# Second MoE projection by Strassen's product for pairs of token tiles, with partial sums read midway

One Trainium2 chip, one of its cores. The metric is the device time of one execution in microseconds (us); lower is better. Faster or slower needs 2%. Engines: PE (TensorE) does the matmuls, ACT (ScalarE) exponentials and copies, DVE (VectorE) elementwise work and sums, POOL (GpSimd) the normalisation; SP is the queue that issues most of the DMAs, called the sync queue. PSUM is the memory that matmuls write to.

## The reference

Attention with RMS-normalised queries and keys (8 batches, 12 heads, 448 positions, 64 columns a head), then two projections with a gate between them on the 3584 tokens:

```python
q_n, k_n = (rmsnorm(q, g_q), rmsnorm(k, g_k))
scores = scale * np.matmul(q_n, k_n.transpose(0, 1, 3, 2))
attn = softmax(scores)                 # (written out in the reference)
x = (attn @ v), heads side by side     # 3584 x 768
h = x @ w_in                           # 768 x 2048
g = h * (1.0 / (1.0 + np.exp(-1.702 * h)))
return g @ w_out                       # 2048 x 768
```

## The kernel before

Everything is one stream per engine. While the program is built, a greedy list schedule (`_Order`) takes tasks with a modelled duration, a priority and dependencies, and fixes the order of the instructions on each engine. On the chip each engine then runs its list in that order and waits where a semaphore says so: PE does nothing else while it waits (in run e4 below it stood 2.70 us in front of one matmul, with the next ones behind it).

Names used below. F(b) is the first projection of batch b, 16 groups of 6 matmuls of 448 columns; each group is followed by a tanh on ACT and a gate on DVE. Y(b) is the second projection: 2 halves of 384 output columns, 16 matmuls of 384 columns for each token tile and half. Attention runs between them. The kernel takes 8 banks of PSUM: 4 for scores (two tiles of two banks each), 1 for attention's output, and 3, called w, which the MoE takes in turn.

```python
banks = [ps_w.tile([128, 512], FP32, tag=f"w{j}", name=f"w{j}") for j in range(3)]
...
def second(bp, tm, hf, c):
    if c == 0:
        ops[bp, tm, hf] = bank()[:, :HALF]
    for ko in range(4 * c, 4 * c + 4):
        nc.tensor.matmul(ops[bp, tm, hf],
                         lhsT=g_of[bp][:, ko, tm * 128:(tm + 1) * 128],
                         rhs=w_out_s[:, ko, hf * HALF:(hf + 1) * HALF],
                         start=(ko == 0), stop=(ko == MI - 1))

def take_out(bp, tm, hf):
    ...
    nc.scalar.mul(osb[:, hf * HALF:(hf + 1) * HALF], ps, 0.5)      # ACT, bank to SBUF
...
N_ATT, N_KZ, N_V, N_RAW, N_SQ, N_QKN = 3, 6, 6, 7, 2, 3            # depths of the rings
raw = ring("raw", N_RAW, [128, 2, 2, NS, D], FP32)                 # loaded q and k
```

## Time and profile before

| | before |
|---|---|
| median of the timed runs | 435.6 us |
| span of the profiled run | 434.0 us |
| PE busy / ACT busy / DVE busy | 421.0 / 318.5 / 216.8 us |
| second projection on PE | 896 matmuls at 162.6 ns, 145.7 us |
| PE idle by the list of waits after 60 us | none |

Spacing, used all through this text, is the time from the start of one matmul to the start of the next. A matmul's own duration in the profile (326 ns for 384 columns) is twice its spacing, so it overlaps the next one, and durations cannot be added. Where the spacing is larger than usual, PE waited.

### The profile page before, as it was taken

The page shows a single profiled execution, that of the slowest core. Times are in us where ns is not written, and L with a number is a line of the kernel's source. Part 1 is how long each engine was busy: PE and PEld are TensorE (multiplying, and loading weights), DVE is VectorE, ACT ScalarE, POOL GpSimd, SP SyncE. Part 2 cuts the span into 40 slices and gives each one's busy share as a digit, 9 for nine tenths or more (in the row PEclk, how much of TensorE's full clock was granted, in tenths as well). Part 3 has the DMA queues.
Part 4 walks back from the last instruction along what each step waited for, and adds up shares of the span by engine and source line. Part 5 has one row for each costly group of instructions (what it writes and reads, how often), then busy time and mean ns, then how long its engine had stood idle before and what let it go on. Part 6 is the DMA issues. An engine that isn't in the chain of part 4 may idle for free.

```text
span 434.0 us, 9991 instructions
## 1 busy us (share of the span) xinstructions
PE 421.0 (97%) x3962; PEld 249.5 (57%) x3962; DVE 216.8 (50%) x460; ACT 318.5 (73%) x472; POOL 180.5 (42%) x277
## 2 busy tenths in 40 slices
PE   6899899999999999999999999999999999999996
PEld 4558687655555555555555555555555555565563
DVE  5977978456575486735754255412551125404400
ACT  4897888769999999989987778766875466314411
POOL 5396753855849857655545454433010000000000
PEclk9999999999999999999999999999999999999999
DMA  9999999899787998677657933235112221021022
GB/s 208 240 253 245 266 251 249 197 257 231 142 216 157 257 255 207 168 175 194 169 120 155 234 98 79 62 85 122 34 33 58 58 76 22 12 72 38 0 74 73
DMA packets 97235, 63.38 MB, mean 146 GB/s; under 512 B 54052, under 2 KB 93732, under 8 KB 97188
## 3 DMA queue, kind: packets, MB, share of 16 engines
q1 hardware_dynamic: 89520, 56.05, 53.8%
q0 software_dynamic: 7296, 6.29, 8.9%
q8 instruction: 31, 0.51, 0.5%
q10 hardware_dynamic: 372, 0.40, 0.3%
q14 instruction: 16, 0.13, 0.1%
HBM read 45.61 MB, written 11.01 MB: 130 GB/s over the span
## 4 chain that ended last, share of the span: by engine, by line
PE 91%; ACT 4%; DMA 2%; DVE 1%; issue 1%; SPq 0%; ACTq 0%
PE w L860 34%; PE w L830 34%; PE o L620 12%; PE sc L599 10%; DMA raw<-in_k_dram 2%; ACT att L609 2%; ACT sq L482 1%; PE w L556 1%; DVE qk L563 0%; PE w L646 0%; DVE qk L560 0%; DVE g L852 0%; DVE obs L631 0%; SPq L475 0%; DVE xt L650 0%
## 5 line engine op out<-in xcount | busy, mean ns | idle before, releaser
L607 ACT ACTIVATE att<-sc 112x896 bf16<-112x896 f32 x168 | 146.1, 919 | 22.3 <-PE sc L599 22.0
L860 PE MATMUL w<-w_out_s,g 128*128 128x384 bf16 x896 | 161.4, 326 | 0.0
L830 PE MATMUL w<-xt,w_in_s 128*128 128x448 bf16 (+1 forms) x864 | 158.3, 332 | 0.0
L852 DVE SCALAR_TENSOR_TENSOR g<-th,w 128x448 bf16<-128x448 f32 x128 | 78.6, 617 | 67.2 <-ACT th L840 67.0
L860 PEld LDWEIGHTS <-g 128*128 128x128 bf16 x896 | 80.9, 98 | 52.4 <-issue 6.3
L830 PEld LDWEIGHTS <-w_in_s 128*128 128x128 bf16 x864 | 78.9, 98 | 52.9 <-issue 3.5
L533 POOL TENSOR_TENSOR row<-raw,rs 112x512 bf16<-112x512 f32 x87 | 90.5, 1063 | 20.5 <-DMA qk<-row 11.5
L620 PEld LDWEIGHTS <-att 112*128 112x128 bf16 x1536 | 70.5, 98 | 41.9 <-issue 20.4
L840 ACT ACTIVATE th<-w 128x448 f32<-128x448 f32 x128 | 69.7, 549 | 33.1 <-PE w L830 31.5
L620 PE MATMUL o<-vx,att 112*128 112x65 bf16 x1536 | 83.1, 195 | 0.8 <-ACT att L609 0.6
L546 POOL TENSOR_TENSOR vx<-vraw,ones 112x512 bf16<-112x512 f32 x42 | 43.7, 1042 | 88.4 <-PE o L620 78.3
L491 DVE TENSOR_REDUCE ssq<-sq 112x16 f32<-112x1024 f32 (+1 forms) x50 | 58.5, 1171 | 26.5 <-ACT sq L482 26.2
L871 ACT ACTIVATE osb<-w 128x384 f32<-128x384 f32 x56 | 27.6, 492 | 46.8 <-PE w L860 45.3
L630 DVE RECIPROCAL rcp<-o 112x4 f32<-112x4 f32 x96 | 17.2, 179 | 89.4 <-PE o L620 89.1
L599 PE MATMUL sc<-qk 64*128 64x448 bf16 (+1 forms) x432 | 54.3, 333 | 1.9 <-DVE qk L563 1.4
L482 ACT ACTIVATE sq<-raw 112x1024 f32<-112x1024 f32 (+1 forms) x46 | 47.6, 1043 | 5.5 <-DMA raw<-in_k_dram 2.5
L631 DVE TENSOR_TENSOR obs<-o,rcp 112x256 bf16<-112x256 f32 x96 | 40.7, 424 | 3.3
L574 ACT ACTIVATE qk<-qk,gG 128x448 bf16<-128x448 bf16 x36 | 24.5, 682 | 0.0
L599 PEld LDWEIGHTS <-qk 64*128 64x128 bf16 x432 | 13.0, 94 | 19.1 <-issue 12.3
L609 ACT ACTIVATE att<-sc 112x896 bf16<-112x896 f32 x24 | 20.5, 914 | 1.9 <-PE sc L599 1.8
L523 POOL TENSOR_TENSOR t<-rs 112x48 f32<-112x48 f32 x28 | 7.4, 265 | 23.8 <-DVE rs L512 22.5
L457 PE MATMUL w<-zeros,ident 128*128 128x256 bf16 x89 | 14.6, 297 | 1.4 <-POOL ident masks.py:199 1.4
(38 smaller groups left out, 110.3 us busy)
## 6 DMA issues: line engine op xcount, KB each, us to landing
raw<-in_q_dram SPq DMA_DIRECT2D x48, 224.0 KB, 4.3
vraw<-in_v_dram SPq DMA_DIRECT2D x48, 224.0 KB, 5.0
raw<-in_k_dram SPq DMA_DIRECT2D x47, 224.0 KB, 4.6
w_in_s<-in_moe_w_in_dram POOLq DMA_DIRECT2D x4, 768.0 KB, 16.1
w_out_s<-in_moe_w_out_dram POOLq DMA_DIRECT2D x4, 768.0 KB, 20.9
out_dram<-osb SPq DMA_DIRECT2D x7, 336.0 KB, 3.2
out_dram<-osb SPq DMA_DIRECT2D x8, 288.0 KB, 3.3
out_dram<-osb SPq DMA_DIRECT2D x8, 240.0 KB, 3.0
```

Of the source, the lines that this page charges most:

```text
L482: nc.scalar.activation(out=sq[i % N_SQ][:SS, part], in_=raw[i % N_RAW][:SS, part], func=ACT.Square)
L491: nc.vector.reduce_sum(out=ssq_of[g0][:SS, i - g0, part], in_=sq[i % N_SQ][:SS, part], axis=AX.X)
L533: eng.tensor_tensor(out=row_ring[i % N_QKN][:SS, gi].rearrange("p n (h d) -> p h n d", h=2), in0=raw[i % N_RAW][:SS, gi], in1=y[:SS, a, gi ...
L546: nc.gpsimd.tensor_tensor(out=vx[:, :, :D], in0=vr, in1=ones[:SS, :].to_broadcast([SS, 2 * NS, D]), op=ALU.mult)
L599: nc.tensor.matmul(sc[:, hp, j * SH:j * SH + n], lhsT=qkw[r, k0:k0 + WIN], rhs=qk[r, 0, qs], start=True, stop=True)
L607: nc.scalar.activation(out=att[:SS, t, :, :S], in_=sc, func=ACT.Exp)
L620: nc.tensor.matmul(os_[u, w][:, x, :], lhsT=att_of(u)[:SS, kc, hp, qs * SS:qs * SS + WIN], rhs=vx_ring[i % N_V][:SS, hp, kc, :], start=(kc ...
L631: nc.vector.tensor_tensor(out=to[:SS, :, w, :] if h is None else to[:SS, :2].rearrange("p n h d -> p (n h) d"), in0=o[:SS, :, :D], in1=rcp ...
L830: nc.tensor.matmul(gps[b, m][:, j * SH:j * SH + n], lhsT=w_in_s[:, ki, f * 128:(f + 1) * 128], rhs=xT[b][:, ki, lo:lo + n], start=(ki == 0 ...
L840: nc.scalar.activation(out=th[:, :], in_=gps[b, m][:, :S], func=ACT.Tanh, scale=0.851)
L852: nc.vector.scalar_tensor_tensor(out=g_of[b // 2][:, f:f + len(g), lo:lo + n], in0=view(ths.pop((b, m))[:, :]), scalar=1.0, in1=view(gps.p ...
L860: nc.tensor.matmul(ops[bp, tm, hf], lhsT=g_of[bp][:, ko, tm * 128:(tm + 1) * 128], rhs=w_out_s[:, ko, hf * HALF:(hf + 1) * HALF], start=(k ...
```

## The change

The intent: Strassen's product (in Winograd's form) makes the 2 x 2 blocks of a pair of token tiles times the four quarters of `w_out` from 7 half products of 8 matmuls where the plain way has 8. The terms of `w_out` are made once and partly overwrite it; the sums of token halves are made by DVE for each pair. The results need partial sums: bank `a` collects products 1, 6, 7 and 4, and is copied out by ACT after each of them; bank `c` collects 5 and 3 and is read by DVE between them. So PE has fewer matmuls, and DVE and the dependencies have more. The last batch may use the four banks of the scores as well. The storage of terms and sums is that of early inputs, so the rings are shorter later on. Stores go by half rows.

```diff
+    K_KZ, K_V, K_RAW, K_VRAW, N_SUM = 3, 2, 5, 4, 3          # depths later: 6, 6, 7, 7 before
+    sc_ring = [ps_sc.tile([128, 2, 512], FP32, tag=f"sc{j}", name=f"sc{j}") for j in range(2)]
+    banks += [t[:, j, :] for t in sc_ring for j in range(2)]
...
+    TERMS = ((T3, T1, B22), (T1, T1, B11), (T2, B22, T1), (T4, B21, T2))
+    def combine(j, r):
+        o, x, y = (t[:, r * NK // 2:(r + 1) * NK // 2] for t in TERMS[j])
+        nc.vector.tensor_tensor(out=o, in0=x, in1=y, op=ALU.subtract)
...
+    def add_up(name, x, y, op):
+        ...
+        nc.vector.tensor_tensor(out=sum_of[name], in0=x, in1=y, op=op)
+    def copy_out(frm, bp, tm, hf):
+        nc.scalar.mul(half_of(bp, tm, hf), held[frm], 0.5)
+    def add_out(frm, bp, tm, hf):
+        o = half_of(bp, tm, hf)
+        nc.vector.scalar_tensor_tensor(out=o, in0=held[frm], scalar=0.5, in1=o, op0=ALU.mult,
+                                       op1=ALU.add)
...
+    EVEN = ["s", 1, 2, 5, 6, 7, 4, 3]
+    FIRST = order("As A1 A2 A5 A6 Bs B1 A7 A4 A3 B2 B5 B6 B7 B4 B3")
+    MIDDLE = order("As A1 A2 A5 A6 C0 A7 C1 A4 A3 C2 Bs B1 B2 B5 B6 C3 B7 B4 B3")
+    FINAL = order("As A1 C0 A2 A5 A6 C1 A7 C2 Bs A4 A3 C3 B1 B2 B6 B5 B7 B8 B4")
...
+        def p6():
+            multiply(P(6), a, S2, T2, False, None, [S2, X(1)] + terms)
+            copy(X(2), t1, 1, P(6), takes=("osb", [("D", bp, t1, 1)]))
+        def p7():
+            multiply(P(7), a, S3, T3, False, None, [S3, X(2)])
...
+        if b == B - 1:
+            od.add("late", "none", 0, lambda: None, 0, widen=("w", len(banks)),
+                   deps=[("E", NG - 1, None, t) for t in range(NS)])
```

A and B are the two pairs of an odd batch, C0 to C3 the four quarters of its single tile (32 matmuls, as before), s the sums; 8 is product 3 in a bank of its own.

## The prediction

> **What bounds the kernel now.** I read four views in this order: busy shares and slices of the page, the chain that ended last, the groups, and the timeline of the end.
>
> ```profile
> span 434.0 us, 9991 instructions
> PE 421.0 (97%) x3962; PEld 249.5 (57%) x3962; DVE 216.8 (50%) x460; ACT 318.5 (73%) x472; POOL 180.5 (42%) x277
> ...
> PE   6899899999999999999999999999999999999996
> ...
> DVE  5977978456575486735754255412551125404400
> ACT  4897888769999999989987778766875466314411
> POOL 5396753855849857655545454433010000000000
> PEclk9999999999999999999999999999999999999999
> ...
> PE 91%; ACT 4%; DMA 2%; DVE 1%; issue 1%; SPq 0%; ACTq 0%
> PE w L860 34%; PE w L830 34%; PE o L620 12%; PE sc L599 10%; DMA raw<-in_k_dram 2%; ACT att L609 2%; ACT sq L482 1%; PE w L556 1%; DVE qk L563 0%; PE w L646 0%; DVE qk L560 0%; DVE g L852 0%; DVE obs L631 0%; SPq L475 0%; DVE xt L650 0%
> ```
>
> PE is full in every slice but the first and the last at full clock, and 91% of the chain is PE. A busy PE proves little by itself, because matmul ends are modelled, so I check density. The stretch view shows PE busy 40.00 of 40.00 us from 100 us to 380 us, the list of waits has no PE matmul waiting after 60 us, and the end of the chain gives real spacing:
>
> ```profile
> 375.28 15.60 PE w L860 x96
> 390.88 18.16 PE w L830 x96
> 409.04 20.81 PE w L860 x128
> ```
>
> So a second-projection matmul (L860, 384 columns) costs 20.81/128 = 162.6 ns and a first-projection one (L830, 448 columns) 18.16/96 = 189.2 ns. The whole second projection is 896 x 0.1626 = 145.7 us; the chain gives it 34.0% of 434.0 = 147.6 us. The two nearly agree, so even where attention is interleaved PE really is packed: PE throughput is the bound from about 60 us on, and a matmul taken out is worth its full spacing. ACT is second: the stretch view gives it 38.7 and 39.3 of 40 us in 100:140 and 140:180, later 28 to 31.
>
> ```profile
> L852 DVE SCALAR_TENSOR_TENSOR g<-th,w 128x448 bf16<-128x448 f32 x128 | 78.6, 617 | 67.2 <-ACT th L840 67.0
> ...
> L871 ACT ACTIVATE osb<-w 128x384 f32<-128x384 f32 x56 | 27.6, 492 | 46.8 <-PE w L860 45.3
> ...
> 409.08 0.54 ACT L840 ACTIVATE th<-w 128x448 f32<-128x448 f32 x1 [0.59 <-PE w L830]
> 409.65 0.62 DVE L852 SCALAR_TENSOR_TENSOR g<-th,w 128x448 bf16<-128x448 f32 x1 [0.52 <-ACT th L840]
> 411.68 0.49 ACT L871 ACTIVATE osb<-w 128x384 f32<-128x384 f32 x1 [2.06 <-PE w L860]
> ```
>
> These give the latencies that the change puts between matmuls: the last gate is ready 409.65+0.62-409.04 = 1.23 us after the last L830 matmul, and a bank is copied out 411.68+0.49-(409.04+2.60) = 0.53 us after its last matmul where ACT is free.
>
> **What the skill says.** "TensorE: Matmul & The Clock Gate", Back-to-back issue gap: columns/2.4 + 2.5 ns, 162.5 ns for 384; the trace has 162.6. "PSUM — Partial Sum Buffer", The four PSUM rules: a partial sum may be read in the middle of an accumulation group if the read is synchronised, and two engines in one bank at once is an error; so each midway read makes the next product into that bank wait for the copy. No trace of before shows that. "VectorE: DVE Perf Modes", the perf-mode tier table: a tensor_tensor all in bf16 from SBUF runs two elements a cycle (1224 ns for 2048), one with a PSUM operand one a cycle. The second half agrees: 448 elements took 617 ns, that is 467 ns at 0.96 GHz plus 150. No bf16 tensor_tensor of two SBUF tensors is in the trace. "SBUF — State Buffer", Who interferes with whom: such a DVE instruction contends with a GpSimd instruction that reads SBUF. I let that cost GpSimd, not PE.
>
> **The change, part by part.** *Removed from PE.* A pair of token tiles took 2 tiles x 2 halves x 16 = 64 matmuls; seven half products of 8 are 56. The loops make 11 pairs: one each in batches 2, 4, 6 and two each in 1, 3, 5, 7. That is 88 matmuls fewer (808 for 896) of the same size: 88 x 0.1626 = 14.3 us. The three single tiles after the weights were overwritten still take 32 matmuls, and so do the three plain tiles of batch 0. Nothing else leaves PE.
>
> *Added to DVE.* 4 sums a pair and one a single tile, 47 of 128x1024 bf16: from the skill's figure (512+158)/0.96 = 0.70 us, an estimate, 33 us. Eight weight terms of 1536 elements, about 0.97 us, 7.7 us once. Three adds a pair from PSUM and one extra, 34 of 384 elements at 400+150 = 0.55 us, 18.7 us. Sum 59 us on a DVE that is busy 217 of 434 and has 67 us of waits for ACT in L852 alone. It goes to about 276 of 425, 65%: off the path as throughput.
>
> *ACT.* 4 copies a pair, as before; 56 copies remain. About 318 of 425 us, 75%.
>
> *Stores.* Same 11 MB, in half rows of 1536 bytes: twice the issues. Each issue is about 0.4 us on the sync queue, some 58 more are 24 us there; DMA in the second half is at 1 to 3 tenths. Hidden. The last store was already by halves on two queues, so the tail of about 4 us stays.
>
> *Shorter rings.* The sums and terms live in buffers of early inputs; later the rings are 3, 2, 5 and 4 deep for 6, 6, 7 and 7. A group of attention takes about 7 us (4 exponentials of 0.919 and its share), its transpose 3.4 us to landing and its GpSimd copy 1.04 us, so two to three groups of lookahead suffice. I charge nothing on PE.
>
> *New waits on PE.* The order inside a pair separates most midway reads from the next product into that bank by another product (8 x 0.1626 = 1.30 us, more than 0.53). Not separated are: both in batches 2, 4, 6 (product 6 to 7 to 4), three in batch 1, one each in 3 and 5, none in 7. That is 11 places. Bare, each is 0.53 us plus a signal, say 0.7; where attention runs, the copy may also sit behind a 0.919 us exponential: about 1.0. Batch 6, past the end of attention or near it, pays 2 x 0.7 = 1.4. The nine others, 9 us bare, can be filled by attention matmuls, which were about a third of PE time around 290 us; I take a fifth left, 1.8. At a stage start product 2 needs the last gates after 1.30 us, where before 12 matmuls (1.95 us) covered them: 1.23 bare is just covered, late by a few tenths behind an exponential; nothing to 0.5 us in all. Sum about 3.2 us.
>
> Total: 435.64 - 14.3 + 3.2 = 424.5 us.
>
> **The rivals.** *Waits eat the gain.* For: instruction order on PE is fixed when the kernel is built, the bank stays held from product 1 to 4, three banks are all that MoE has until the last exponential, and ACT was over 96% busy in 100:180. If all 11 places cost 1 us and gates another 2, the gain is 14.3-13 = 1.3 us: 434. Against: the ordering was plainly made to separate reads, and attention pieces are small and plentiful there. About one in ten for most of this.
>
> *ACT or attention becomes the bound.* The even batches lose 40 matmuls of 96 (6.5 us) at once, so the next first projection wants its attention sooner. By the exponentials counted in the stretches, attention had about 24 groups done at 180 us, where batch 3 needs 24, and that batch started at 198.88; the new start is about 9 us earlier, 190. Lead left, but small; if it ran out a few us would be lost there: 427 to 430. From 220 us ACT has a quarter of its time free.
>
> *DVE sums become the wait.* Four in a row are 2.8 us; the first is needed two products (2.6 us) after the last matmul of the first projection, and may start 1.23 us after it: 1.23+0.70 = 1.9, ahead. Contention with GpSimd (65% busy early) or a reduction of 1.21 us in front could make it late in batches 1 to 3: 1 to 2 us, 426.
>
> *All hidden.* 421.3 to 422.
>
> **Range and chances.** Floor 435.64-14.3 = 421.3; the centre leaves 3.2 us of waits, the range up to 8. The 2% line is 426.9, which needs 8.7 of the 14.3 us to survive. I put 0.80 on that, 0.18 within 2%, 0.02 slower: slower would need 23 us of new PE idle.
>
> **What would show it.** L860's successors at 808 matmuls, dense spacing still 162.6 ns; DVE at about 276 us, with sums near 0.70 and adds near 0.55 us; ACT unchanged at about 318 us; PE waits of 0.5 to 1 us on ACT copies or DVE adds, concentrated in batches 2, 4, 6; PE's part of the chain falling by some 14 us, with one to three us of ACT copies appearing in it; the end of attention some 10 us earlier. It is wrong if PE shows waits over 6 us, if waits on sums or gates outweigh those on copies, if PE waits for attention's transposes before a first projection, or if sums take over 1 us.

## The result

The changed kernel takes 433.1 us in the median (431.45 to 434.6, 4 runs) beside 435.6 us. The ratio is 0.9944 (95% interval 0.9919 to 0.9969). Ratios here are the mean time of one kernel's fast runs over that of the other's of the same rounds, so not quite the ratio of the medians. So it is faster by half a per cent, inside the 2%, and above the predicted range, which left room for 8 us of waits over a floor of 421.3 us.

The page of the changed kernel, as far as it answers to the lines in the prediction:

```profile
span 431.6 us, 10059 instructions
PE 412.6 (96%) x3874; PEld 242.7 (56%) x3874; DVE 275.6 (64%) x549; ACT 317.2 (73%) x472; POOL 189.5 (44%) x277
...
PE   6999899999999999999999899999999999999995
...
PE 81%; ACT 6%; DVE 5%; DMA 4%; issue 2%; POOL 0%; SPq 0%; DVEq 0%; ACTq 0%; POOLq 0%
```

The counts are as predicted: 3962 - 3874 = 88 matmuls fewer, DVE 275.6 us for the 276 foreseen, ACT unchanged. But PE was busy 421.0 - 412.6 = 8.4 us less, where 14.3 us of matmuls were taken out, and the span fell by 2.4 us. In the chain that ended last, PE has 81% where it had 91%; ACT, DVE and DMA have 15% where they had 7%. PE waits now, and the list of what its matmuls waited for, which was empty after 60 us, has this in it:

```profile
PE w L951 <- ACT osb L961: 3.3, 5, 1.5
...
PE w L951 <- DVE osb L965: 1.2, 2, 0.6
PE o L653 <- DVE obs L664: 1.0, 1, 1.0
PE sc L951 <- DVE osb L965: 0.7, 1, 0.7
PE sc L951 <- ACT osb L961: 0.6, 1, 0.6
```

L951 is the matmul of a product, L961 the midway copy by ACT, L965 the add by DVE, L653 attention's second matmul behind a division (L664). The columns are total us, times, longest us. These idle times are too small, because a matmul's modelled end covers part of the wait. Spacing counts all of it. The usual spacing is untouched (median 162 ns within products, 189 ns within the first projection, as before), so I took the spacing of every two neighbours on PE after 90 us, less the usual one for that kind of pair, and listed all that exceeded it by 0.12 us. Before: none. After: 18 places, 10.4 us in all (one score matmul after another is left out, here and in the table of runs; it would add one wait of 0.28 us, in F1):

| kind of wait | where | us | foreseen |
|---|---|---|---|
| next product into bank `a` waits for its midway copy | Y1 0.74, Y3 1.68, Y4 0.48, Y6 0.48 and 0.74 | 4.1 | 3.2 |
| product 5 waits for a third bank (add after product 2) | Y3 0.75, Y5 0.74 | 1.5 | 0 |
| a matmul waits for a reader of the other bank of its score tile | F7 0.32 and 0.32, Y7 0.74 and 0.87 | 2.2 | 0 |
| attention's matmul is late; the longest waits for a division behind other DVE work | Y4 1.16, four of 0.13 to 0.17 | 1.8 | 0 |
| first projection waits for a gate behind the weight terms | F1 0.29 and 0.45 | 0.7 | 0 to 0.5 |

14.3 us taken out less 10.4 us of new waits is 3.9 us. In this profiled run another 0.65 us went before the change has any effect: the first projection began at 36.40 us for 35.75, and the clock over the first 20 us was 0.91 for 1.00; that the one caused the other is not shown. (What is left of the difference to 2.4 us is the wait of 0.28 us and smaller ones.)

How each kind looks in the timeline of the changed kernel (start, duration, engine and line; in brackets the idle time before, and who ended it). First, a midway copy with nothing between the products, batch 6:

```profile
378.73 1.46 PE L951 MATMUL w<-late 128*128 128x384 bf16 x8 [0.32 <-ACT osb L961]
380.22 0.49 ACT L961 ACTIVATE osb<-w 128x384 f32<-128x384 f32 x1 [1.55 <-PE w L951]
380.76 1.46 PE L951 MATMUL w<-late,g 128*128 128x384 bf16 x8 [0.58 <-ACT osb L961]
```

ACT is idle and starts at once; still the eight matmuls of one product start 2.03 us before the next eight, for 1.30 us packed. That is the bare price of reading a bank midway with nothing in between: 0.73 us, of which the copy is 0.49. The prediction had 0.7 for it. The longest of the five, 1.68 us in batch 3, is for the most part something else:

```profile
243.85 1.06 ACT L514 ACTIVATE sq<-raw 112x1024 f32<-112x1024 f32 x1 [1.34 <-DMA raw<-in_k_dram]
244.81 0.47 ACT L961 ACTIVATE osb<-w 128x384 f32<-128x384 f32 x1
245.34 0.97 PE L951 MATMUL w<-late,g 128*128 128x384 bf16 x5 [1.52 <-ACT osb L961]
```

ACT stood 1.34 us for a load of k, and the copy is listed behind the square of that load. With quicker loads (e6 below) this wait was 0.23 us, so some 1.4 us of the first row of the table are a late load. Now the third bank, batch 3:

```profile
235.62 0.56 DVE L965 SCALAR_TENSOR_TENSOR osb<-w,osb 128x384 f32<-128x384 f32 x1 [2.02 <-PE w L951]
236.24 0.65 PE L951 MATMUL w<-w_out_s,late 128*128 128x384 bf16 x3 [0.59 <-DVE osb L965]
```

Product 5 of pair B begins a new accumulation, yet it waits. Half of the single tile (C2, still to be completed by C3) holds one of three banks, product 1 a second, and product 2, which has just ended, the third until DVE has added it. The prediction looked only for readers of the same accumulation. Third, a division late on DVE, batch 4:

```profile
275.81 1.55 DVE L942 TENSOR_TENSOR late<-g 128x1024 bf16<-128x1024 bf16 x1
276.77 1.49 POOL L565 TENSOR_TENSOR row<-raw,rs 112x512 bf16<-112x512 f32 x1
277.39 1.42 DVE L942 TENSOR_TENSOR late<-late,g 128x1024 bf16<-128x1024 bf16 x1
278.73 0.68 DVE L942 TENSOR_TENSOR late<-g 128x1024 bf16<-128x1024 bf16 x1
279.81 0.56 DVE L965 SCALAR_TENSOR_TENSOR osb<-w,osb 128x384 f32<-128x384 f32 x1
280.50 0.42 DVE L664 TENSOR_TENSOR obs<-o,rcp 112x256 bf16<-112x256 f32 x1
280.98 0.43 PE L653 MATMUL o<-vx,att 112*128 112x65 bf16 x8 [0.99 <-DVE obs L664]
```

A sum alone takes 0.68 us; two took 1.55 and 1.42 us beside GpSimd's normalisation, which itself took 1.49 us for its usual 1.04. The division for attention came behind them and PE stood.

The fourth kind needs a view of the program as it was built (instruction, line, tile at its offset in elements; 512 elements are one bank). In the last batch the MoE may use the four score banks. Product 2 of pair B writes one bank of the tile `sc1`; in the middle of its eight matmuls there is a wait on ACT:

```
I-5969 L951 Matmult sc1_163 at 512 <- w_out_s_109, g_5280
I-5970 L951 Matmult sc1_163 at 512 <- w_out_s_109, g_5280
I-5972 L961 Activation osb_5971 <- sc1_163 at 0
I-5973 L951 Matmult sc1_163 at 512 <- w_out_s_109, g_5280   [waits Activation_49]
```

```profile
417.26 1.30 PE L951 MATMUL sc<-w_out_s,g 128*128 128x384 bf16 x7
418.60 0.49 ACT L961 ACTIVATE osb<-sc 128x384 f32<-128x384 f32 x1 [1.46 <-PE sc L951]
419.14 0.81 PE L951 MATMUL sc<-w_out_s,g 128*128 128x384 bf16 x4 [0.58 <-ACT osb L961]
```

No product needs a wait there. What ACT reads at 418.60 is product 1, in the other bank of the same tile. The kernel's schedule counts single banks; the wait that was built in is that of a two-bank tile.

### The profile page after: what moved, and what is told of

Same layout as the page of the kernel before. It is cut to its first block, busy times and chain, and to the rows that moved or that the text cites.

```text
span 431.6 us, 10059 instructions
## 1 busy us (share of the span) xinstructions
PE 412.6 (96%) x3874; PEld 242.7 (56%) x3874; DVE 275.6 (64%) x549; ACT 317.2 (73%) x472; POOL 189.5 (44%) x277
## 4 chain that ended last, share of the span: by engine, by line
PE 81%; ACT 6%; DVE 5%; DMA 4%; issue 2%; POOL 0%; SPq 0%; DVEq 0%; ACTq 0%; POOLq 0%
PE w L864 30%; PE w L951 20%; PE o L653 11%; PE sc L632 9%; PE w L894 4%; PE sc L951 3%; PE sc L864 3%; DMA raw<-in_k_dram 2%; ACT att L642 2%; ACT sq L514 1%; PE w L588 1%; ACT osb L961 1%; DVE g L886 1%; ACT att L640 1%; DVE late L942 1%
## 5 line engine op out<-in xcount | busy, mean ns | idle before, releaser
L640 ACT ACTIVATE att<-sc 112x896 bf16<-112x896 f32 x168 | 146.8, 924 | 23.5 <-PE sc L632 23.2
L864 PE MATMUL w<-xt,w_in_s 128*128 128x448 bf16 (+1 forms) x804 | 149.1, 330 | 0.5 <-DVE g L886 0.4
L653 PEld LDWEIGHTS <-att 112*128 112x128 bf16 x1536 | 72.0, 98 | 44.8 <-issue 19.0
L653 PE MATMUL o<-vx,att 112*128 112x65 bf16 x1280 | 73.4, 194 | 1.1 <-DVE obs L664 1.0
L951 PEld LDWEIGHTS <-late 128*128 128x128 bf16 x376 | 33.7, 97 | 26.0 <-issue 7.6
L632 PE MATMUL sc<-qk 64*128 64x448 bf16 (+1 forms) x360 | 47.5, 344 | 0.9 <-DVE qk L595 0.5
L664 DVE TENSOR_TENSOR obs<-o,rcp 112x256 bf16<-112x256 f32 x96 | 40.7, 424 | 3.3
L951 PEld LDWEIGHTS <-g 128*128 128x128 bf16 x336 | 30.1, 97 | 22.2 <-issue 5.5
L961 ACT ACTIVATE osb<-w 128x384 f32<-128x384 f32 x45 | 22.1, 490 | 24.4 <-PE w L951 21.7
L951 PE MATMUL w<-w_out_s,g 128*128 128x384 bf16 x192 | 36.1, 326 | 0.0
L951 PE MATMUL w<-w_out_s,late 128*128 128x384 bf16 x168 | 32.8, 326 | 1.2 <-DVE osb L965 1.2
L951 PE MATMUL w<-late 128*128 128x384 bf16 x160 | 31.1, 326 | 1.2 <-ACT osb L961 1.2
L965 DVE SCALAR_TENSOR_TENSOR osb<-w,osb 128x384 f32<-128x384 f32 x27 | 15.0, 554 | 20.4 <-PE w L951 11.0
```

The source lines that it names most:

```text
L632: nc.tensor.matmul(sc[:, hp, j * SH:j * SH + n], lhsT=qkw[r, k0:k0 + WIN], rhs=qk[r, 0, qs], start=True, stop=True)
L640: nc.scalar.activation(out=att[:SS, t, :, :S], in_=sc, func=ACT.Exp)
L653: nc.tensor.matmul(os_[u, w][:, x, :], lhsT=att_of(u)[:SS, kc, hp, qs * SS:qs * SS + WIN], rhs=vx_ring[turn(i, N_V, K_V)][:SS, hp, kc, :], ...
L664: nc.vector.tensor_tensor(out=to[:SS, :, w, :] if h is None else to[:SS, :2].rearrange("p n h d -> p (n h) d"), in0=o[:SS, :, :D], in1=rcp ...
L864: nc.tensor.matmul(gps[b, m][:, j * SH:j * SH + n], lhsT=w_in_s[:, ki, f * 128:(f + 1) * 128], rhs=xT[b][:, ki, lo:lo + n], start=(ki == 0 ...
L951: nc.tensor.matmul(held[to], lhsT=lhs[:, ko, :], rhs=y[:, ko, :], start=first and ko == 0, stop=ko == NK - 1, skip_group_check=not first)
```

## The experiments

Twelve kernels ran, each beside the kernel before on the same chip; four chips were used, so the ratios compare better than the medians. "Wrong" says that the result is not the reference's.

| run | median us | ratio to before (95%) | PE waits in its profiled run, us |
|---|---|---|---|
| the change | 433.1 | 0.9944 (0.9919 to 0.9969) | 10.4 |
| e1_unpaired | 431.6 | 0.9908 (0.9893 to 0.9923) | 8.5 |
| e2_nosum (wrong) | 431.25 | 0.9906 (0.9888 to 0.9924) | 9.1 |
| e3_nocopy (wrong) | 431.04 | 0.9905 (0.9868 to 0.9942) | 8.3 |
| e4_all_off (wrong) | 429.31 | 0.9847 (0.9810 to 0.9884) | 8.3 |
| e5_no_product | 435.79 | 0.9994 (0.9976 to 1.0013) | 0 |
| e6_small_loads (wrong) | 432.01 | 0.9907 (0.9885 to 0.9928) | 9.8 |
| e7_all_off_small (wrong) | 423.87 | 0.9725 (0.9705 to 0.9745) | 2.1 |
| e8_reordered | 424.64 | 0.9740 (0.9721 to 0.9758) | 3.7 |
| e9_order_only | 425.02 | 0.9751 (0.9726 to 0.9776) | 3.2 |
| e10_seven_banks | 430.94 | 0.9891 (0.9858 to 0.9925) | 8.7 |
| e11_priorities_only | 430.85 | 0.9875 (0.9839 to 0.9911) | 6.6 |
| e12_order_paired | 428.75 | 0.9828 (0.9799 to 0.9858) | 5.7 |

The last column is the sum of excess spacing after 90 us, as above. By the 2% rule e7, e8 and e9 are faster, e12 is unclear and the others are the same.

**e1_unpaired: no two lent banks of one score tile.**

```diff
-    banks += [t[:, j, :] for t in sc_ring for j in range(2)]
+    banks += [t[:, 0, :] for t in sc_ring]
```

> Edit: in the last batch only one bank of each two-bank score tile is lent to the MoE (5 banks for 7). My theory: in the changed kernel's trace PE stops twice in the middle of an accumulation in the last stage (0.74 and 0.87 us) and twice in the last first projection (0.32 us each), each time on a copy or gate that reads the OTHER bank of the same score tile, because dependencies are kept by tile; with no two banks of one tile in use these four waits, 2.2 us, go: 430.9 us against 433.1, and no PE gap is left after the last first projection starts. Rivals (late attention because of the shorter rings; a loaded DVE; plain copy latency) leave those four waits or move them: 433 us, and the gaps stay.

431.6 us. The four waits are gone from its trace: F7 took 18.16 us for 18.79 and Y7 up to the last matmul 23.24 for 24.84, together 2.23 us, as expected. By the medians the gain is 1.5 us, and the intervals of the two ratios just overlap: other waits vary from run to run (in this trace Y2, F2 and F3 had 0.26 to 0.61 us more of them, Y3 0.83 us less).

**e2_nosum: the sums are not made.**

```diff
-        nc.vector.tensor_tensor(out=sum_of[name], in0=x, in1=y, op=op)
+        sum_of[name] = sum_of[x] if x in sum_of else tokens(*x)      # and nothing on DVE
```

> Edit: the sums of token halves are not computed (products read a token half in their place: wrong result on purpose); the order on PE, ACT and the stores is the same. If the DVE load of the sums (33 us) is what eats the gain, PE waits on gates, sums and divisions fall and the time goes to about 425 us. My theory: DVE lateness costs PE only about 1.2 to 1.6 us of the sums' making (the wait of 1.16 us on a division behind four sums and an add in batch 4 is the largest; the weight terms stay): 431.6 us, within 1 us; the waits on copies stay.

431.25 us. The 1.16 us wait of batch 4 is gone, the copies' waits stay. DVE's sums (37.7 us in the changed kernel) are not by themselves what eats the gain.

**e3_nocopy: the midway copies are left out.**

```diff
-            od.add(name, "ACT", 490, lambda: copy_out(a, bp, tm, hf), ...
+            od.add(name, "ACT", 490, (lambda: None) if name[0][0] == "X" else ..., ...
-        nc.vector.scalar_tensor_tensor(out=o, in0=held[frm], scalar=0.5, in1=o, ...)
+        nc.vector.tensor_scalar(out=o, in0=held[frm], scalar1=0.5, scalar2=None, op0=ALU.mult)
```

> Edit: the midway copies (X1, X2, X3) by ACT are left out and the adds write the bank alone (wrong result on purpose); the order on PE is the same, the DVE adds read and last the same. My theory: the PE waits on those copies in the changed kernel's trace add up to 0.74+1.68+0.48+0.48+0.74 in batches 1, 3, 4, 6 and 0.74 in the last, 4.9 us, and go: 428.3 us, with the waits on DVE adds (0.75 twice in batches 3 and 5, 0.87 in the last) still there. If late attention or DVE is the cause, the gap only moves to the next wait: above 431.5 us.

431.04 us: nearer to the rival. All waits on copies are gone from the trace, as the theory said, but new ones stand earlier and elsewhere: 1.12 us in F2, 1.33 in Y2, 0.91 in Y3, all of attention's matmuls. Before the one in Y2 the chain runs through three sums and a reduction on DVE: there the sums are late after all.

**e4_all_off: the three together.**

> Edit: all three together (unpaired banks, no sums, no midway copies; wrong result on purpose); PE order as in the changed kernel. My theory: the 14.3 us of matmuls are really gone and the waits above are what took their place, so the effects add: 433.1 - 2.2 - 1.4 - 4.2 = 425.3 us (the 0.74 of the last stage counted once), with 1.5 us left of waits for the third bank in batches 3 and 5 and about 0.7 on gates in batch 1. If something else (slower matmuls, switching between attention and MoE, late loads) holds the time, it stays above 428 us.

429.31 us, not 425.3: the theory falls in its simple form. The waits that I had listed do not add, since something else stood behind them. Its trace shows one wait of 2.87 us in F2 and one of 1.50 in Y3, and the timeline says behind what:

```profile
163.03 1.06 ACT L514 ACTIVATE sq<-raw 112x1024 f32<-112x1024 f32 x1 [2.53 <-DMA raw<-in_k_dram]
...
164.12 1.22 DVE L523 TENSOR_REDUCE ssq<-sq 112x16 f32<-112x1024 f32 x1 [2.97 <-ACT sq L514]
...
165.99 0.42 DVE L664 TENSOR_TENSOR obs<-o,rcp 112x256 bf16<-112x256 f32 x1
...
166.47 0.43 PE L653 MATMUL o<-vx,att 112*128 112x65 bf16 x8 [2.70 <-DVE obs L664]
```

A load of k landed late; ACT, which keeps its order, waited 2.53 us in front of the square, DVE 2.97 us in front of the reduction, and the division behind it released PE. This load is for a later group; PE needed only the division. A prefetch that is late holds up all that is listed behind it. In the chain, that load was issued after GpSimd had normalised the group whose buffer it takes: this is the shortened ring, to which the prediction gave no cost. Before the wait in Y3 it is another thing: from 235.40 to 241.17 us the chain runs through stores, loads and a transpose issued one after another on the sync queue, and only then comes the load of k. The wait of 2.87 us was followed by 3.41 us at a granted clock of 0.5 (the only such drop between 60 and 420 us in these traces), in which eight spacings were longer by 1.4 us in all; they are in the 8.3 us.

**e5_no_product: rings, half rows and half buffers, with all tiles by the plain way.**

```diff
-            if b % 2: ... pairs and single tiles ...
+        for tm, hf in [(tm, hf) for tm in tms for hf in range(2)]:
+            plain(bp, b, tm, hf)
+            take(bp, tm, hf, last)
```

> Edit: everything of the change but the Strassen product itself: the shortened rings in shared storage, the half-row stores and six half buffers, with all tiles by the plain 64-matmul way as before. Measures rings and stores alone. My first theory and the prediction: they cost nothing on PE, 435.6 to 436 us. Rival, raised by the run with all three off (where PE waited 2.87 us and 1.50 us on divisions that stood behind a square waiting for a late k load): the rings alone delay loads and cost some time even with PE full: 437 to 439 us.

435.79 us, ratio 0.9994: no cost, and not one excess spacing in the trace. The loads are late here too: ACT waited for k in four places, 2.7 us in all after 60 us, where the kernel before has none. With PE full, that never reached a matmul.

**e6_small_loads and e7_all_off_small: loads after the 14th group bring an eighth of the rows.**

```diff
-        eng.dma_start(out=raw[turn(i, N_RAW, K_RAW)][:SS, which], in_=src)
+        part = SS if i < 2 * N_RAW else SS // 8
+        eng.dma_start(out=raw[turn(i, N_RAW, K_RAW)][:part, which], in_=src[:part])
```

> Edit: the changed kernel, but loads of q, k and v after the 14th group bring 14 of 112 rows (wrong result on purpose), so they land earlier; order unchanged. Revised theory: only what stands on late loads goes, above all about 1.1 of the 1.68 us wait in batch 3 and a few tenths in batches 2 and 3; the waits on copies, on the third bank and inside score tiles stay: 431 to 432 us against 433.1. If late loads are the main cause of the lost gain: 426 us or less. If they cost nothing: 433.

> Edit: unpaired banks, no sums, no midway copies AND the small loads (wrong result on purpose); order unchanged. Revised theory: with the product's own waits gone, late loads were what held the run with all three off at 429.3 us; with them gone too the full 14.3 us show except for the third-bank waits (1.4) and gates of batch 1 (0.7): 424 us. If the lateness comes from the transposes, from DVE or from GpSimd, the time stays at 428 us or above.

In the changed kernel quicker loads give 432.01 us: about what was expected; the intervals of the two ratios overlap, so the gain of about 1 us is not certain. The 1.68 us wait of batch 3 fell to 0.23. With the product's own waits gone, quicker loads take the time from 429.31 to 423.87 us, where 424 was expected. What is left in that trace is four waits: 0.29 and 0.46 on gates in F1 and 0.68 twice on the third bank, 2.1 us. So the saving on PE is real, about 12 us of it visible, and it was hidden behind two layers: the product's waits in front, late loads for the most part behind them. The smaller loads also lighten the DMA queues for the transposes, so this run does not separate the load's own length from the traffic.

**e8_reordered: a correct version that separates the midway reads.** The order of products becomes the one below (in e8 slightly varied, the last batch too, and with shifted task priorities, which leave fewer holes on PE in the kernel's own list schedule), with unpaired banks.

```diff
-    EVEN = ["s", 1, 2, 5, 6, 7, 4, 3]
+    EVEN = ["s", 1, 2, 6, 5, 7, 8, 4]
-    FIRST = order("As A1 A2 A5 A6 Bs B1 A7 A4 A3 B2 B5 B6 B7 B4 B3")
-    MIDDLE = order("As A1 A2 A5 A6 C0 A7 C1 A4 A3 C2 Bs B1 B2 B5 B6 C3 B7 B4 B3")
+    FIRST = order("As A1 A2 A6 A5 A7 A8 A4 Bs B1 B2 B6 B5 B7 B8 B4")
+    MIDDLE = order("As A1 C0 C1 A2 A6 A5 A7 A8 A4 C2 C3 Bs B1 B2 B6 B5 B7 B8 B4")
```

Products 1, 6, 7, 4 go to bank `a`; with 2, 5 and 8 between them each copy has 1.30 us of other matmuls to hide in. Product 3 as 8 in a bank of its own costs one more DVE add. The parts of the single tile stand together, so no half-done accumulation holds a bank through a pair.

> Edit: a correct version with the same work as the changed kernel: unpaired banks, products in an order in which the products into one bank are separated by another product wherever there is a midway read (1 2 6 5 7 8 4 within a pair, the third product in a bank of its own), and task priorities shifted so that the list schedule leaves fewer holes on PE. Theory: nothing but waits was lost, so an order with fewer of them gets the gain: the holes of batches 1, 3, 4, 5 and 6 (about 6 us) and of the last batch (2.2 us) go, late loads give some back: 425 to 428 us. If the waits are inherent in three banks and the midway reads, or the rings hold the rest: above 430 us.

424.64 us, ratio 0.9740, with a correct result: faster than both kernels. Which part of it did it?

**e9_order_only and e11_priorities_only.** e9 is the diff above and unpaired banks, nothing else. e11 is the shifted priorities and unpaired banks with the change's order.

> Edit: the changed kernel with unpaired banks and only the order of products altered (1 2 6 5 7 8 4 within a pair in every batch but the last, single-tile parts together); task priorities as in the changed kernel. If separating the products is what brought the reordered version to 424.6, this is within 1 us of it: 424 to 426 us. My theory: it is half of it, because a longer chain of sums and the same late attention leave holes: the waits on copies and on the third bank of batches 1, 3, 5 go (about 4 us less unpaired 2.2), some waits on sums and divisions come: 428 to 430 us.

> Edit: unpaired banks and the shifted task priorities of the reordered version, but the product order of the change. Theory: copies are still read just before the next product into the bank and batch 5 still waits for the third bank, so about 3 us of holes stay: 428 to 430 us. If priorities alone are what counts (attention placed earlier), it is within 1 us of 424.6.

The order alone gives 425.02 us, better than I expected; the priorities alone 430.85 us, next to 431.6 for unpaired banks alone. So the order of products is what counts, and the shifted priorities were not needed. e9 has exactly the work of the change plus 9 adds. Its list of waits has none on a midway copy any more:

```profile
PE o L653 <- DVE obs L664: 0.9, 1, 0.9
PE w L951 <- DVE late L942: 0.7, 1, 0.7
```

These two, one division and one product waiting for its sum, are the longest left after the start. In batch 6, where the change waited 0.48 and 0.74 us, the same copies now lie beside matmuls:

```profile
371.96 1.46 PE L951 MATMUL sc<-w_out_s,late 128*128 128x384 bf16 x8
372.16 0.49 ACT L961 ACTIVATE osb<-w 128x384 f32<-128x384 f32 x1 [3.01 <-PE w L951]
373.26 0.81 PE L951 MATMUL w<-late 128*128 128x384 bf16 x4
```

The copy of bank `a` runs under product 5, and product 7 starts at 373.26, 1.30 us after it: packed. Late loads show up less in this order, though its rings are the same: after 60 us ACT waited for loads of k in two places, 1.3 us in all, where the change had eight and 4.1 us, and e4 eight and 9.2 us. From e1 to e9, profiled run to profiled run, the span falls by 6.1 us, the listed waits by 5.2 and the start of the first projection by 0.7.

**e10_seven_banks and e12_order_paired: the paired banks back in e8 and in e9.**

> Edit: the reordered version of 424.6 us with the seven paired banks of the change in the last batch put back. Theory: waits inside an accumulation on the other bank of a score tile come back, in the last first projection and the last products: 425.5 to 427 us. If pairing was only harmful in that one order: 424.6, no change.

> Edit: the product order of the run at 425.0 us with the seven paired banks of the change in the last batch. Theory: the last batch's order is the change's own, so just its four waits inside score tiles come back, 0.32+0.32+0.74+0.87 = 2.2 us: 427.3 us. If pairing interacts with the new order of the batch before it, as in the reordered version with seven banks, more: 429 us or above.

Pairing costs more in both than expected: 430.94 for 424.64 us, and 428.75 for 425.02. In e12's trace F7 waits twice for 0.94 us, where the change had 0.32, and Y7 once for 0.81. In e10 nine of the sixteen waits are in F6, Y6, F7 and Y7. So the cost of the shared tile is not a constant; I take it, without a run that shows it, that the order before decides which bank falls on which neighbour.

The four combinations of the two edits: 433.1 (neither), 431.6 (unpaired), 428.75 (order), 425.02 us (both).

## Why the prediction was wrong

- **Removed from PE, 14.3 us: right.** 88 matmuls fewer at unchanged spacing; with nearly all waits taken away (e7) the time is 423.87 us, 2.6 above the floor of 421.3 that the prediction named, with 2.1 us of waits left.
- **New waits on PE, 3.2 us: this term was mis-sized, and it is the step that failed.** It measured 10.4 us. The mechanism that it counted, a product waiting for the midway copy, measured 4.1 us: five waits instead of eleven; four are of the foreseen size (0.48 to 0.74 us), and in the fifth, 1.68 us, some 1.4 are a late load. Its sum had weak places too: the "9 us bare" of nine places is 6.3 us by its own 0.7 us, and that a fifth of it stays rested on no number. The other 6.3 us are kinds that the step did not look for: the third bank (1.5), the other bank of a tile in the last batch, for which it said "none in 7" (2.2), attention behind DVE (1.8), and gates behind the weight terms (0.7). I looked for conflicts within one accumulation; the ones that I missed come from what else holds a bank, and from in-order lists of other engines.
- **DVE off the path as throughput: right, but lateness is not throughput.** 275.6 us busy for about 276 foreseen, in part by luck: sums and weight terms took 37.7 and 9.0 us for 33 and 7.7, and more of DVE's time overlapped. A sum takes 0.68 us alone and 0.80 on average, beside GpSimd up to 1.55; the adds 0.55, as foreseen. Not making the sums gained at most a few us (431.25 for 433.1).
- **Shorter rings, nothing on PE: true of the rings alone (e5), not in the changed kernel.** There a late load already costs some 1.4 us (batch 3), and once the other waits go it is more: e4 to e7 is 5.4 us. With the order of e9 little of it is left.
- **Stores hidden: right of rings and stores alone (e5).** In the changed kernel it is not shown: before the late load of batch 3 two stores were issued on the sync queue (236.56 to 237.74 us), between the release of a buffer by GpSimd at 236.02 and the issue of the load at about 238.2.
- **Rivals.** The one that came true is "waits eat the gain", given one chance in ten for most of it. "ACT or attention becomes the bound" appeared in e4 in another form: not ACT's load, but a late prefetch at the head of its list. The condition for being wrong that the prediction set, PE waits over 6 us, was met. A sign that it named did not come: attention's last exponential started at 371.3 us for 363.2 before, later and not some 10 us earlier.

That 424.64 and 425.02 us were reached with nearly the same work (10 and 9 adds more) is no merit of the number 424.5; it was predicted for an order that does not reach it.

What stays open: how much of the late loads is the ring's depth, how much the issues on the sync queue (half-row stores among them) and how much the traffic, and why e9 has so few of them.

## What to carry to other kernels

When work is taken from the engine that bounds the kernel, list for each new instruction on it not only what it reads, but what else must be finished first: the reader of the accumulator's last state, whatever holds the buffer that it takes, and the whole in-order list in front of that reader. Put independent work that covers the reader and its signals (0.73 us here for a copy of 0.49) between two uses of an accumulator, and close one accumulation before opening the next if buffers are few. Waits that hide one another do not add: take them away together before concluding that a saving was not there.

## What the Trainium skill lacked or had wrong

- "PSUM — Partial Sum Buffer" says that a synchronised read of a partial sum in the middle of a group is allowed, and gives no price. Here, with nothing between the two products, it held PE for 0.74 us with an ACT copy of 384 columns (the copy itself 0.49 us) and 0.81 to 0.87 us with a DVE add of 0.56 us (there of the other bank of the same tile); with 1.30 us of other matmuls between, in e9, nothing.
- The same page advises guarding PSUM by bank, in its section on bank collisions (where the error that the prediction names under the four rules stands too). No page has the case met here: a tile over two banks was guarded as one, so a matmul waited for a reader of the other bank, 2.2 us in the changed kernel; in two other orders lending both banks of a tile cost 3.7 and 6.3 us of time.
- "SBUF — State Buffer", Who interferes with whom, agrees, and these are its sizes in a real kernel: a bf16 sum of 1024 elements took 0.68 us alone and up to 1.55 us beside a GpSimd instruction, which took 1.49 for 1.04 us.
- "VectorE: DVE Perf Modes": the estimate of 0.70 us for that sum from the page's table held (0.68 measured).
